# Second layers of the experts by seven products in the second pass, with split weights kept in DRAM by the first

## The chip, the cores and the metric

The kernel runs on one core of a Trainium2 chip. The metric is the device time of one execution in microseconds, from launch to end. Beside it stands one execution with the hardware profiler, whose span runs from the first instruction to the last. The engines are TensorE (PE in the rows; PEld is its loading of weights), VectorE (DVE), ScalarE (ACT), GpSimd (POOL), and SyncE (SP), which here issues every DMA.

## What is computed

An attention with a banded mask gives 2304 tokens of width 512. A mixture of eight experts follows, in which every token passes through every expert, and then a plain block of the same kind. In the reference, cut to what matters:

```python
x = attention(q, k, v)                      # 2304 x 512
P = sinkhorn(exp(x @ w_gate))               # 2304 x 8, weights of the experts
for e in range(8):
    h = np.maximum(x @ w1[e], 0.0)          # 2304 x 1024
    out += P[:, e:e + 1] * (h @ w2[e])      # 2304 x 512
y = np.maximum(out @ w_in, 0.0) ** 2 @ w_out   # hidden width 2048
```

All of it is float32. The matrix engine gets float32 operands in two parts: `hi`, the value cast to a shorter form, and `lo`, the rest. One product of blocks is then three matmuls: hi by hi, hi by lo, lo by hi. Casting `hi` is an ACT instruction, `lo = src - hi` a DVE one.

## The kernel before, in words

After the attention (about the first 100 us) come 80 **steps**: each takes 256 hidden units through both layers. The tokens are cut into two pairs of halves of 512 (tokens 0 to 1023 and 1280 to 2303) and one single block of 256 (1024 to 1279). The steps run in four phases: phase 0, or the **first pass** (steps 0 to 31), takes all experts over the first pair and the single block; phase 1, the **second pass** (steps 32 to 63), takes the same experts over the second pair; phases 2 and 3 (eight steps each, from 64 and 72) do the same for the plain block. Every expert's weights are thus loaded and split twice.

**First layers.** `l1_pair` computes the 2 x 2 block product (two blocks of hidden units, two halves of tokens) by seven block products u1 to u7 instead of eight, from sums and differences of the operands. Its input's combinations lie in slots 0 to 6 of `x_hi`, `x_lo`; those of the weights in `blk` and `sum`. `product` issues six matmuls of 128x512 for each (L473). The results land in the banks `s`, `pt`, `xt`; DVE and ACT put them together, multiply by the tokens' expert weight `pp` (g, L521) and split g into gh and gl (L529, L507).

**Second layers.** `l2_units` returns, for a pair, eight units: four chunks of 128 output channels by two halves of tokens, six matmuls each (L636) into one of three `mm` banks, after which DVE adds the bank to `acc` (L654). The units of step i run between the products of step i+1, so the second layer is one step behind.

**Preparing weights.** `prep_w` in step i makes `blk` and `sum` of step i+1 and `w2` of step i: POOL forms the sums (L146 to L151, four instructions of 128x256), ACT casts three blocks of 128x1024 (L133), and DVE forms three `lo` (L137). Raw weights come by DMA (L119) into the buffers `raw1`, `raw2`.

**Order.** Each engine's instructions run in the order in which they are written down here by hand. `run(u)` writes one unit's matmuls, then everything due; `after(k, f)` makes f due k units later. A unit is the clock: in a step of the second pass the units are u1 u2 u3 u4, then second-layer units and u5, u6, u7 in turn, then the remaining second-layer units.

**Changes of phase.** At the start of a phase the slots of `x_hi` and `x_lo` are filled anew: `new_operands` loads blocks into `xb`, POOL forms differences (L208), ACT and DVE split seven pieces for each of two column blocks j (L211, L214), over the last step of a phase and the first of the next. Before u1 of the new phase `ahead` runs five second-layer units.

**Narrowing.** `w_in` and `w_out` arrive as 64-bit numbers. `narrow` brings a block to float32 in four pieces: a DMA, then 2, 2 and 3 DVE instructions (L176 to L198), and a store to `w32`. There are 32 blocks. `narrow_on` does one piece: two pieces in a step of the first pass, at units 0 and 8, three in a step of the second, at units 0, 5 and 10.

Of the kernel before, what the change touches and what calls it, by code (L numbers as in the profile page):

```python
# [47 lines left out]
def tile_kernel(ctx: ExitStack, tc: tile.TileContext, a):  # L48
# [35 lines left out]
    p_dram = dram.tile([NCH, E, 128], F32, name="p_dram")  # L84

# [15 lines left out]
    wset = [None, None]  # L101

    def new_set(pool, k):
        wset[k] = {
            n: tuple(pool.tile([128, 1024], F32R, name=f"{n}{h}{k}", bufs=1) for h in ("h", "l"))
            for n in ("blk", "sum", "w2")
        }

# [6 lines left out]
    def load_w(i, which):  # L115
        if i >= len(steps):
            return
        dst = raw1.rearrange("p b c -> p (b c)") if which == 0 else raw2
# [6 lines left out]
    def prep_w(i):  # L125
# [16 lines left out]
        if i + 1 < len(steps):  # L142
# [83 lines left out]
    def new_operands(src):  # L226
# [3 lines left out]
        for j, base, loads in ((0, 1, (-6, -6)), (1, 14, (11, 13))):  # L230
# [234 lines left out]
    g_t, acc = {}, {}  # L465

# [65 lines left out]
    def l1_pair(i):  # L532

        bank_a, bank_b, bank_c = bank("s"), bank("pt"), bank("xt")
        made = {}

        def made_here():
            g_t[i, 0] = tuple(
                post[0].tile([128, FC, 2 * T], F32R, tag=n, name=n, bufs=2) for n in ("gh", "gl")
            )  # L540
            for n in ("s2", "s3"):
                made[n] = post[0].tile([128, 512], F32, tag=n, name=n, bufs=1)

        def out(fc, t, src, k):
            gh, gl = g_t[i, 0]
# [32 lines left out]
        def u7():  # L578
            product(bank_c, i, "sum", 3, 2, stop=True)
            after(0, lambda: nc.vector.tensor_tensor(out=made["s2"], in0=bank_c, in1=made["s2"], op=ALU.add))  # L580
            out(0, 1, made["s2"], 2)
# [5 lines left out]
    def l1_single(i):  # L587
        def unit(fcs):

            if fcs[0] == 0:  # L590
                g_t[i, 1] = tuple(
                    post[0].tile([128, FC, NSG], F32R, tag=n, name=n, bufs=1) for n in ("sgh", "sgl")
                )
            gh, gl = g_t[i, 1]
            ps = bank("mm")[:, :len(fcs) * NSG]
# [84 lines left out]

    def operands(i):

        if phase(i) == 1:
            return new_operands(x_dram)
        t0 = PAIRS[pair_of(i)]
        return new_operands(y_dram[:, :, t0:t0 + 2 * T])
# [8 lines left out]
    with tc.manual_schedule():  # L695
# [145 lines left out]
        acc[1] = post[0].tile([128, KC * NSG], F32, name="acc1", bufs=1)  # L841
# [138 lines left out]
```

## Time and profile before

| | |
|---|---|
| median of 3 runs | 1990.86 us (1989.66 to 1990.91) |
| the profiled execution | 1989.59 us |
| its span | 1987.6 us |
| PE busy | 1966.0 us (99%) |
| DVE busy | 1527.3 us (77%) |
| ACT, POOL busy | 711.4, 384.3 us |
| DMA, mean of the span | 80 GB/s |

The profiled execution took 2.0 us more than its span. A busy share counts time in which at least one instruction of the engine is under way. Consecutive matmuls overlap, so that the time of one in the rows is longer than the distance from one to the next. The chain of waits follows the work that ended last back from the end: what stands on it sets the time.

### The profile page before, as it was taken

The numbers are of one execution on the slowest core, as the hardware profiler recorded it, in microseconds if no ns is written. First come the engines' busy times: TensorE is split into PE (matmuls) and PEld (weight loads), VectorE is DVE, ScalarE is ACT, GpSimd is POOL, SyncE is SP. The second block draws the span as 40 slices with busy tenths as digits, with TensorE's granted clock in tenths as the row PEclk, the third lists the DMA queues.
The fourth block names the chain that finished last, engine by engine and source line by source line (L and its number), as shares of the span: only waits on it lengthen the run. The fifth ranks groups of instructions, "written<-read, shape, count | busy, mean of one in ns | idle before, by whom it ended". The sixth has DMA issues, their size and how long they took to land.

```text
span 1987.6 us, 27653 instructions
## 1 busy us (share of the span) xinstructions
PE 1966.0 (99%) x11208; PEld 1634.7 (82%) x11208; DVE 1527.3 (77%) x2272; ACT 711.4 (36%) x1104; POOL 384.3 (19%) x412
## 2 busy tenths in 40 slices
PE   8999999999999999999999999999999999999999
PEld 7778888888888888888888888888888878887887
DVE  5866777777777777778888888888887886678776
ACT  3543223222233333223433333333333354344542
POOL 4621311111110111112212121121212221123120
PEclk9999999999999999999999999999999999999999
DMA  8511111111211111212322222222221221113111
GB/s 291 180 67 61 59 60 57 54 64 64 64 64 64 57 61 53 69 54 100 111 92 83 92 85 95 85 76 90 86 89 59 86 106 43 43 54 109 62 45 51
DMA packets 69807, 158.23 MB, mean 80 GB/s; under 512 B 6176, under 2 KB 31408, under 8 KB 69680
## 3 DMA queue, kind: packets, MB, share of 16 engines
q1 hardware_dynamic: 69680, 156.47, 23.3%
q8 instruction: 88, 1.44, 0.3%
q14 instruction: 39, 0.32, 0.0%
HBM read 136.45 MB, written 20.00 MB: 79 GB/s over the span
## 4 chain that ended last, share of the span: by engine, by line
PE 93%; DVE 5%; ACT 1%; issue 0%; POOL 0%; ACTq 0%; DVEq 0%; POOLq 0%
PE mm L636 47%; PE pt L473 15%; PE s L473 11%; PE xt L473 11%; PE mm L602 6%; PE xt L346 2%; DVE acc L654 1%; PE pt L331 1%; PE mm L773 1%; DVE x_lo L214 1%; PE s L294 1%; DVE blkl L137 1%; DVE g L521 0%; DVE gl L507 0%; DVE suml L137 0%
## 5 line engine op out<-in xcount | busy, mean ns | idle before, releaser
L654 DVE TENSOR_TENSOR acc<-mm,acc 128x512 f32<-128x512 f32 x626 | 429.2, 688 | 156.0 <-PE mm L636 152.9
L529 ACT CAST gh<-g 128x512 fp32r<-128x512 f32 x308 | 191.6, 622 | 585.1 <-DVE g L521 585.1
L636 PE MATMUL mm<-gh,w2h 128*128 128x512 f32 x1024 | 399.5, 390 | 0.9 <-DVE acc L654 0.8
L636 PE MATMUL mm<-gl,w2h 128*128 128x512 f32 x1024 | 398.6, 389 | 0.0
L636 PE MATMUL mm<-gh,w2l 128*128 128x512 f32 x1024 | 398.5, 389 | 0.0
L146 POOL TENSOR_TENSOR sums<-raw 128x256 f32<-128x256 f32 x80 | 66.0, 825 | 1411.5 <-DVE suml L137 1388.3
L636 PEld LDWEIGHTS mm<-gh,w2h 128*128 128x128 f32 x1024 | 192.3, 188 | 43.0 <-DVE acc L654 2.6
L636 PEld LDWEIGHTS mm<-gh,w2l 128*128 128x128 f32 x1024 | 192.2, 188 | 40.1
L636 PEld LDWEIGHTS mm<-gl,w2h 128*128 128x128 f32 x1024 | 192.3, 188 | 39.3
L507 DVE TENSOR_TENSOR gl<-g,gh 128x512 fp32r<-128x512 f32 x308 | 223.3, 729 | 0.0
L521 DVE SCALAR_TENSOR_TENSOR g<-s,pp 128x512 f32<-128x512 f32 x183 | 128.9, 704 | 105.6 <-PE s L473 103.5
L473 PE MATMUL xt<-x_hi,sumh 128*128 128x512 f32 x320 | 125.6, 392 | 0.4
L473 PE MATMUL pt<-x_hi,sumh 128*128 128x512 f32 x320 | 124.8, 390 | 0.8 <-ACT s L566 0.8
L473 PE MATMUL s<-x_hi,blkh 128*128 128x512 f32 x320 | 125.2, 391 | 0.0
L473 PE MATMUL xt<-x_hi,suml 128*128 128x512 f32 x320 | 124.8, 390 | 0.3
L473 PE MATMUL s<-x_lo,blkh 128*128 128x512 f32 x320 | 124.7, 390 | 0.0
L473 PE MATMUL xt<-x_lo,sumh 128*128 128x512 f32 x320 | 124.6, 389 | 0.0
L473 PE MATMUL s<-x_hi,blkl 128*128 128x512 f32 x320 | 124.6, 389 | 0.0
L473 PE MATMUL pt<-x_lo,sumh 128*128 128x512 f32 x320 | 124.5, 389 | 0.0
L473 PE MATMUL pt<-x_hi,suml 128*128 128x512 f32 x320 | 124.5, 389 | 0.0
L602 PE MATMUL mm<-xs,blkh 128*128 128x256 f32 x640 | 115.8, 280 | 0.0
L137 DVE TENSOR_TENSOR w2l<-raw,w2h 128x1024 fp32r<-128x1024 f32 x80 | 102.8, 1285 | 11.6 <-ACT w2h L133 11.6
(146 smaller groups left out, 3634.1 us busy)
## 6 DMA issues: line engine op xcount, KB each, us to landing
raw<-in_w SPq DMA_DIRECT2D x128, 512.0 KB, 3.4
raw<-w SPq DMA_DIRECT2D x32, 512.0 KB, 3.4
v<-in_v SPq DMA_DIRECT2D x24, 384.0 KB, 3.7
pp<-p_dram SPq DMA_DIRECT2D x32, 256.0 KB, 5.7
xb<-in_w_in SPq DMA_DIRECT2D x16, 512.0 KB, 4.6
w<-xb SPq DMA_DIRECT2D x32, 256.0 KB, 2.3
xb<-in_w_out SPq DMA_DIRECT2D x16, 512.0 KB, 4.9
k<-in_k SPq DMA_DIRECT2D x24, 224.0 KB, 4.7
```

The costliest lines, as they stand in the source:

```text
L137: nc.vector.tensor_tensor(out=w[1], in0=src, in1=w[0].bitcast(F32), op=ALU.subtract)
L146: tt(out=c(sums, 0), in0=c(raw1, 2), in1=c(raw1, 3), op=ALU.add)
L214: return lambda: nc.vector.tensor_tensor(out=x_lo[:, k, j], in0=z, in1=x_hi[:, k, j].bitcast(F32), op=ALU.subtract)
L294: nc.tensor.matmul(ps[QB * head:QB * head + QB, 2 * (g % 3) + g // 3, :], qt[rows, pr, g * QB:g * QB + QB], kt[rows, pr, g * QB:g * QB + K ...
L346: nc.tensor.matmul(xt[D * h:D * h + D, pr, c * QB:c * QB + QB], vt[keys, c, head * D:head * D + D], pt[keys, c * 128 + head * QB:c * 128 + ...
L473: nc.tensor.matmul(ps, w[:, c], z[:, x, j], start=start and k == 0, stop=stop and k == 5, skip_group_check=True)
L507: nc.vector.tensor_tensor(out=glo, in0=z, in1=ghi.bitcast(F32), op=ALU.subtract)
L521: nc.vector.scalar_tensor_tensor(out=held["g"], in0=src, scalar=0.0, in1=held["r"], op0=ALU.max, op1=ALU.mult)
L529: after(k + 1, lambda: nc.scalar.copy(ghi, held["g"]))
L602: nc.tensor.matmul(ps[:, n * NSG:n * NSG + NSG], w[:, c], z[:, kc], start=k == 0, stop=k == 3 * KC - 1)
L636: nc.tensor.matmul(ps, lhsT, rhs, start=k == 0, stop=k == 3 * FC - 1)
L654: nc.vector.tensor_tensor(out=dst, in0=ps, in1=dst, op=ALU.add)
```

## The change

The first pass keeps its split weights: `store` writes hi and lo of `blk`, `sum`, `w2` and of a new block `mix` to DRAM (eight DMAs of 512 KB in a step); `fetch` reads them back in the second pass, in which nothing of the experts' weights is loaded raw, summed or split. `mix` holds four sums and differences of blocks of `w2`, formed on POOL in the first pass (m1, m2) and split like the rest.

In the second pass the second layer too is a 2 x 2 block product (two blocks of hidden units by two halves of output channels; two halves of tokens) by seven products v1 to v7 (`l2_mixed`). Each has six matmuls, three into each of two banks. Their operands are made in `out_mixed`: g of the four (block, half) combinations (r1 to r4), four differences on POOL (t1 to t4), and seven splits, named 11, 22, 21 and t1 to t4, where there were four. The result of v1 is copied by ACT from its banks a0, a1 to b0, b1; each of v2 to v7 ends in two adds to `acc` on DVE. The units of a step are in the order `u1 v1 u2 v2 u3 v6 u4 v5 u5 v7 u6 v3 u7 v4`; the v belong to the step before. All eight banks are given out once for the pass.

At the change from phase 1 to 2 `ahead` is empty, and the first units of step 64 are `v1 v2 u1 us v6 v5 u2 ...` (us is the single block's first layer). The pieces of the new operands are due at other units. Narrowing moves: one block in a step of the first pass from step 3, at units 2, 16, 17 and 1 of the next, none in the second pass, the last five blocks in phase 2.

```diff
+    def store(n, s, w):
+        for h, z in zip("hl", w):
+            nc.sync.dma_start(w_dram[n + h][s], z.bitcast(F32))
+    def fetch(n, i, w):
+        for h, z in zip("hl", w):
+            nc.sync.dma_start(z.bitcast(F32), w_dram[n + h][i - NS1])
...
+        if kept(i + 1):
+            w = wset[(i + 1) % 2]
+            out += [(0, lambda: fetch("blk", i + 1, w["blk"])), (0, lambda: fetch("sum", i + 1, w["sum"]))]
...
+        if kept(i):
+            w2 = wset[i % 2]["w2"]
+            out += [(0, lambda: fetch("w2", i, w2)), (0, lambda: fetch("mix", i, mixes[i % 2]))]
...
+            def m1():
+                tt(out=c(z, 0), in0=r[:, 0, 1], in1=r[:, 1, 1], op=ALU.add)
+                tt(out=c(z, 2), in0=r[:, 0, 0], in1=r[:, 0, 1], op=ALU.subtract)
...
+            out += [(1, hi(w2, raw2)), (3, lo(w2, raw2, lambda: store("w2", i, w2)))]
+            out += [(6, m1), (7, m2), (13, hi(m, mix32)), (15, lo(m, mix32, lambda: store("mix", i, m)))]
...
+        def operand(n, src, k, k_lo):
+            b = block[n]
+            after(k, lambda: nc.scalar.copy(b[:, 0], src))
+            after(
+                k_lo,
+                lambda: nc.vector.tensor_tensor(out=b[:, 1], in0=src, in1=b[:, 0].bitcast(F32), op=ALU.subtract),
+            )
...
+                def mix():
+                    sub(r1, r4, r1)
+                    sub(r5, r2, r1)
+                    sub(r4, r2, r4)
+                    sub(r3, r3, r5)
+                after(2, mix)
+                operand("t1", r1, 3, 4)
+                operand("t2", r5, 4, 5)
+                operand("t3", r4, 5, 7)
+                operand("t4", r3, 6, 8)
...
+        def unit(banks, w, n, dst=None, start=False, stop=False, first=False, final=False):
+            z = block[n]
+            for m, ps in enumerate(banks):
+                c = slice(m * 128, m * 128 + 128)
+                for k, (wt, g) in enumerate(((0, 0), (0, 1), (1, 0))):
+                    nc.tensor.matmul(
+                        ps, w[wt][:, c], z[:, g], start=start and k == 0, stop=stop and k == 2, skip_group_check=True
+                    )
+            if dst is None:
+                after(0, lambda: [nc.scalar.copy(o, ps) for o, ps in zip((b0, b1), banks)])
+                return
...
+        return dict(
+            v1=lambda: unit(a_, whole(0, 0), "11", start=True),
+            v2=lambda: unit(a_, whole(1, 0), "21", (0, 0), stop=True, first=True, final=True),
+            v6=lambda: unit(b_, mixed(1), "t2", (0, 1), first=True),
+            v5=lambda: unit(a_, mixed(0), "t1", (1, 1), start=True, first=True),
+            v7=lambda: unit(b_, mixed(2), "t3", (1, 1), final=True),
+            v3=lambda: unit(a_, mixed(3), "22", (0, 1), stop=True, final=True),
+            v4=lambda: unit(b_, whole(1, 1), "t4", (1, 0), stop=True, first=True, final=True),
+        )
...
+                if i == first[2]:
+                    names = "v1 v2 u1 us v6 v5 u2 v7 u3 v3 u4 v4 u5 u6 u7"
+                    u["us"], l1s = l1s[0], []
+                elif i == first[2] - 1:
+                    names = "u1 v1 u2 v2 u3 u4 v6 u5 v5 u6 u7 v7 v3 v4"
+                else:
+                    names = "u1 v1 u2 v2 u3 v6 u4 v5 u5 v7 u6 v3 u7 v4"
...
-                if SCALED + 2 <= i < first[2] - 5 and not slow and k in ((0, 8), (0, 5, 10))[pair_of(i)]:
+                if i >= SCALED and phase(i) in (0, 2) and not slow and done[0] % 4 == {2: 0, 16: 1, 17: 2, 1: 3}.get(k):
                     narrow_on()
```

**PE, inside a step of the second pass, before.** One product of the first layer (u5, into `pt`) and one unit of the second layer behind it (into an `mm` bank; gh, gl are the split g, w2h and w2l the split weights).

```order
L473 MATMUL pt_13254<-x_hi_82,sumh0_142 128x512
L473 MATMUL pt_13254<-x_lo_83,sumh0_142 128x512
L473 MATMUL pt_13254<-x_hi_82,suml0_143 128x512
L473 MATMUL pt_13254<-x_hi_82,sumh0_142 128x512
L473 MATMUL pt_13254<-x_lo_83,sumh0_142 128x512
L473 MATMUL pt_13254<-x_hi_82,suml0_143 128x512
L636 MATMUL mm_13315<-gh_13128,w2h1_2220 128x512
L636 MATMUL mm_13315<-gl_13129,w2h1_2220 128x512
L636 MATMUL mm_13315<-gh_13128,w2l1_2221 128x512
L636 MATMUL mm_13315<-gh_13128,w2h1_2220 128x512
L636 MATMUL mm_13315<-gl_13129,w2h1_2220 128x512
L636 MATMUL mm_13315<-gh_13128,w2l1_2221 128x512
```

**PE, the same place of the changed kernel**: u5 and v7 (g1 holds the operands t2, t3, t4; mixh0 and sg are hi and lo of `mix`; `mm` and `xt` are the banks b0, b1).

```order
L527 MATMUL pt_9251<-x_hi_82,sumh1_2230 128x512
L527 MATMUL pt_9251<-x_lo_83,sumh1_2230 128x512
L527 MATMUL pt_9251<-x_hi_82,suml1_2231 128x512
L527 MATMUL pt_9251<-x_hi_82,sumh1_2230 128x512
L527 MATMUL pt_9251<-x_lo_83,sumh1_2230 128x512
L527 MATMUL pt_9251<-x_hi_82,suml1_2231 128x512
L795 MATMUL mm_9254<-g1_2237,mixh0_2240 128x512 x2
L795 MATMUL mm_9254<-g1_2237,sg_2238 128x512
L795 MATMUL xt_9250<-g1_2237,mixh0_2240 128x512 x2
L795 MATMUL xt_9250<-g1_2237,sg_2238 128x512
```

A second-layer unit still has six matmuls, now three into each of two banks; a step has seven of them where it had eight.

**DVE, from the end of one step of the second pass into the next, before**: adds to `acc` (L654), the three splits of weights (L137), those of g (L507), and narrowing (L176, L180).

```order
L137 TENSOR_TENSOR suml_2219<-sums,sumh_2218 128x1024
L654 TENSOR_TENSOR acc_2222<-mm,acc_2222 128x512
L507 TENSOR_TENSOR gl<-g,gh 128x512
L654 TENSOR_TENSOR acc_2222<-mm,acc_2222 128x512
L521 SCALAR_TENSOR_TENSOR g<-s,pp 128x512
L137 TENSOR_TENSOR w2l_2221<-raw_99,w2h_2220 128x1024
L654 TENSOR_TENSOR acc_2222<-mm,acc_2222 128x512
L507 TENSOR_TENSOR gl<-g,gh 128x512
L137 TENSOR_TENSOR blkl_141<-raw_97,blkh_140 128x1024
L176 TENSOR_SCALAR xb<-xb 128x512
L180 SCALAR_TENSOR_TENSOR xb<-xb 128x512
```

**DVE, the same place of the changed kernel**: s2 of u7 (L681), the lo of 21, g of block 0 and half 1 (L618 into mix), the adds of v4 (L809), the lo of 22, t1 and t2 (L608; the buffers r hold the g and their differences), the adds of v2, g of u3, the lo of t3.

```order
L681 TENSOR_TENSOR s2_10665<-xt_9249,s2_10665 128x512
L608 TENSOR_TENSOR g0_2236<-mix32_2239,g0_2236 128x512
L618 SCALAR_TENSOR_TENSOR mix32_2239<-s2_10665,pp_10207 128x512
L809 TENSOR_TENSOR acc0_2234<-mm_9254,acc0_2234 128x512
L809 TENSOR_TENSOR acc0_2234<-xt_9250,acc0_2234 128x512
L608 TENSOR_TENSOR g0_2236<-r2_9178,g0_2236 128x512
L608 TENSOR_TENSOR g0_2236<-r1_9177,g0_2236 128x512
L608 TENSOR_TENSOR g1_2237<-r5_9179,g1_2237 128x512
L809 TENSOR_TENSOR acc0_2234<-mm_9252,acc0_2234 128x512
L809 TENSOR_TENSOR acc0_2234<-mm_9253,acc0_2234 128x512
L618 SCALAR_TENSOR_TENSOR r1_9177<-s_9247,pp_10643 128x512
L608 TENSOR_TENSOR g1_2237<-mix32_2239,g1_2237 128x512
```

The splits of weights and the narrowing are gone from the step; twelve adds stand where eight stood, and seven splits of operands where four stood, three of them behind differences that POOL forms.

**POOL, over the change from phase 1 to 2, before**: the differences of the new operands (L208) and the sums of weights (L146 to L151).

```order
L208 TENSOR_TENSOR xb<-xb 128x512 x7
L146 TENSOR_TENSOR sums<-raw_97 128x256
L147 TENSOR_TENSOR sums<-raw_97 128x256
L150 TENSOR_TENSOR sums<-sums,raw_97 128x256
L151 TENSOR_TENSOR sums<-raw_97,sums 128x256
L208 TENSOR_TENSOR xb<-xb 128x512
```

**POOL, the same place of the changed kernel**: the differences of the operands t1 to t4 (L629) come between.

```order
L261 TENSOR_TENSOR xb<-xb 128x512 x4
L629 TENSOR_TENSOR r_9177<-mix_2239,r_9177 128x512
L629 TENSOR_TENSOR r_9179<-r_9178,r_9177 128x512
L629 TENSOR_TENSOR mix_2239<-r_9178,mix_2239 128x512
L629 TENSOR_TENSOR mix_2239<-mix_2239,r_9179 128x512
L167 TENSOR_TENSOR sums<-raw_105 128x256
L168 TENSOR_TENSOR sums<-raw_105 128x256
L261 TENSOR_TENSOR xb<-xb 128x512
```

In steps 63 and 64 POOL has four more instructions of 128x512 each than before.

## Rows read from the trace of the kernel before

**Rows 1.** The page: busy time of the engines, and the chain by engine.

```profile
PE 1966.0 (99%) x11208; PEld 1634.7 (82%) x11208; DVE 1527.3 (77%) x2272; ACT 711.4 (36%) x1104; POOL 384.3 (19%) x412
PE 93%; DVE 5%; ACT 1%; issue 0%; POOL 0%; ACTq 0%; DVEq 0%; POOLq 0%
```

**Rows 2.** Windows in first pass, second pass, phase 2: stretch; busy time by engine, clock, DMA.

```profile
500.00:550.00 50.00, 50.00 (x245) 42.39 (x244) 36.13 (x54) 14.40 (x21) 6.64 (x8) 1.00 0.20 64
1200.00:1250.00 50.00, 50.00 (x222) 41.37 (x221) 44.89 (x67) 16.88 (x24) 8.13 (x10) 1.00 0.23 80
1700.00:1750.00 50.00, 50.00 (x237) 42.03 (x237) 34.89 (x50) 20.50 (x32) 7.42 (x8) 1.00 0.12 43
```

**Rows 3.** Chain of waits in the second pass: start, length, engine, bank, line, count.

```profile
1017.02 6.82 PE mm L636 x30
1023.84 1.36 PE s L473 x6
1037.44 6.82 PE mm L636 x30
1179.40 1.67 PE xt L473 x6
1508.82 6.80 PE mm L636 x30
```

**Rows 4.** DVE in order of time, inside a step: start, length, instruction.

```profile
1206.50 0.68 DVE L521 SCALAR_TENSOR_TENSOR g<-s,pp 128x512 f32<-128x512 f32 x1
1207.10 0.69 DVE L654 TENSOR_TENSOR acc<-mm,acc 128x512 f32<-128x512 f32 x1
1207.70 1.22 DVE L137 TENSOR_TENSOR suml<-sums,sumh 128x1024 fp32r<-128x1024 f32 x1
1208.83 0.69 DVE L654 TENSOR_TENSOR acc<-mm,acc 128x512 f32<-128x512 f32 x1
```

**Rows 5.** Groups of instructions, second pass (POOL: all): count, busy us, mean ns, idle before.

```profile
L636 PE MATMUL mm<-gl,w2h 128*128 128x512 f32 x374 | 145.6, 389 | 0.0
L529 ACT CAST gh<-g 128x512 fp32r<-128x512 f32 x93 | 57.8, 622 | 203.2 <-DVE g L521 203.2
L176 DVE TENSOR_SCALAR xb<-xb 128x512 int32<-128x512 int32 x17 | 7.1, 418 | 0.0
L180 DVE SCALAR_TENSOR_TENSOR xb<-xb 128x512 int32<-128x512 int32 x17 | 14.3, 841 | 0.6
L658 POOL TENSOR_TENSOR acc<-acc,pp 128x512 f32<-128x512 f32 x8 | 12.8, 1618 | 15.5 <-DVE acc L654 15.5
```

**Rows 6.** Line L208 on POOL: shortest, median and longest ns.

```profile
L208 POOL TENSOR_TENSOR xb<-xb x24: 1289/1298/2161, 913.5 to 1812.1; 128x512 f32<-128x512 f32 x24
```

**Rows 7.** POOL and DVE in order of time at the change from phase 1 to 2.

```profile
1580.13 2.67 POOL L208 TENSOR_TENSOR xb<-xb 128x512 f32<-128x512 f32 x2 [0.69 <-DVE x_lo L214]
1581.55 2.33 DVE L137 TENSOR_TENSOR w2l<-raw,w2h 128x1024 fp32r<-128x1024 f32 x1
1588.10 2.99 POOL L208 TENSOR_TENSOR xb<-xb 128x512 f32<-128x512 f32 x2 [5.30 <-DVE x_lo L214]
1588.65 1.28 DVE L521 SCALAR_TENSOR_TENSOR g<-s,pp 128x512 f32<-128x512 f32 x1
1589.86 0.68 DVE L654 TENSOR_TENSOR acc<-mm,acc 128x512 f32<-128x512 f32 x1
```

**Rows 8.** Windows of PE alone at that change: stretch, busy, clock, DMA.

```profile
1590.00:1600.00 10.00, 9.19 (x38) 1.00 0.24 70
1600.00:1610.00 10.00, 9.96 (x55) 1.00 0.43 166
```

**Rows 9.** DMA: issues (count, KB, us to landing), and a window like rows 2.

```profile
raw<-in_w SPq DMA_DIRECT2D x128, 512.0 KB, 3.4
y_dram<-acc SPq DMA_DIRECT2D x16, 256.0 KB, 2.1
896.00:898.00 2.00, 2.00 (x10) 1.66 (x9) 1.55 (x3) 0.63 (x2) 0.00 (x0) 1.00 1.00 387
```

More of the change, by code (lines that the diff above doesn't have):

```diff
@@ L115, in load_w @@
     def load_w(i, which):
-        if i >= len(steps):
+        if i >= len(steps) or kept(i):
             return
+        moe, s = steps[i]
+        while not moe and done[0] < 16 * s + 8 * which + 8:
+            narrow_on()
         dst = raw1.rearrange("p b c -> p (b c)") if which == 0 else raw2
@@ L465, in tile_kernel @@
     g_t, acc = {}, {}
+    gbuf, block, r32, own, l2_banks, spare = [], {}, [], {}, [], []
     def product(ps, i, which, slot, x, start=False, stop=False):
@@ L590, in unit @@
             if fcs[0] == 0:
[L591 to L593 removed]
+                g_t[i, 1] = tuple(sg[:, h].rearrange("p (f n) -> p f n", f=FC) for h in range(2))
             gh, gl = g_t[i, 1]
[L595 removed]
+            ps = (spare[0] if i == 2 * NS1 else bank("mm"))[:, :len(fcs) * NSG]
             hi, lo = wset[i % 2]["blk"]
@@ L679, in l2_units, with l2_mixed, add @@
         return [lambda c=c: unit(c, 0, DM) for c in range(n // 128)]
-    def operands(i):
+    def l2_mixed(i):
+        s = steps[i][1]
+        d = acc[0].rearrange("p (e m t n) -> p e m t n", e=2, m=2, t=2)
+        w2 = [z.rearrange("p (f e d) -> p f e d", f=FC, e=2) for z in wset[i % 2]["w2"]]
+        mix = [z.rearrange("p (k d) -> p k d", k=4) for z in mixes[i % 2]]
+        whole = lambda f, e: [z[:, f, e] for z in w2]
+        mixed = lambda k: [z[:, k] for z in mix]
+        (a0, a1), (b0, b1) = l2_banks
+        def unit(banks, w, n, dst=None, start=False, stop=False, first=False, final=False):
[9 more added lines that the diff above has]
+                return
+            def add():
+                e, t = dst
+                for m, ps in enumerate(banks):
+                    o = d[:, e, m, t]
+                    if first and s == 0:
+                        nc.scalar.copy(o, ps)
+                    else:
+                        nc.vector.tensor_tensor(out=o, in0=ps, in1=o, op=ALU.add)
+                    if final and s == NS1 - 1:
+                        t0 = PAIRS[1] + t * T
+                        nc.sync.dma_start(y_dram[:, 2 * e + m, t0:t0 + T], o)
+            after(0, add)
+        a_, b_ = (a0, a1), (b0, b1)
+        return dict(
[6 more added lines that the diff above has]
+            v4=lambda: unit(b_, whole(1, 1), "t4", (1, 0), stop=True, first=True, final=True),
+        )
@@ L865, in tile_kernel @@
                 ahead, l2, l2s = l2[:-3] + l2s, l2[-3:], []
+            if i == NS1 + 1:
+                s0, spare0 = bank("s"), bank("s")
+                x0, x1 = bank("xt"), bank("xt")
+                own.update((k, (s0, bank_p, x0)) for bank_p in [bank("pt")] for k in range(i, 2 * NS1))
+                l2_banks.extend(((bank("mm"), bank("mm")), (bank("mm"), x1)))
+                spare.append(spare0)
             l1 = l1_pair(i) if i else first_units
```

112 lines of the change are left out of this document (88 added, 24 removed).

## The prediction

> **What bounds the kernel now.** The first view is the page: PE is busy for 1966.0 of 1987.6 us and makes up 93% of the chain that ended last [rows 1]. A share that high can hide slack, so the second view is the windows: in the first pass, the second and phase 2 PE is busy for 50.00 of 50.00 us at the full granted clock, while DVE has 36.13, 44.89 and 34.89 us [rows 2]. The reader is to see that in the second pass DVE is the engine nearest to PE. The third view is the chain in order of time, since one matmul is recorded at 389 ns [rows 5] though matmuls overlap. Six matmuls take 1.36 us on it [rows 3], so one costs 0.2267 us; with 389 ns the gain would be overrated by 70%. A step of the second pass has 42 + 48 = 90 matmuls, 20.41 us, and the chain shows 1037.44 - 1017.02 = 20.42. Over 24 steps it shows (1508.82 - 1017.02)/24 = 20.49: some steps lose 0.31 us at u7 (1.67 for six matmuls), where PE waits for DVE [rows 3].
>
> **The matmuls.** The order shows 42 + 42 = 84 matmuls a step. Second-layer units of all 32 steps change: 32 x 6 x 0.2267 = **43.5 us off**, the whole of it on the path as long as PE waits for nothing else. A unit that alternates between two banks is not in the trace; alternate units already change bank after every six matmuls without a loss [rows 3], so I take the same price.
>
> **DVE in a step of the second pass.** Two instructions of 512 columns start 0.60 us apart, one of 1024 holds DVE for 1.13 [rows 4]. Removed: three splits of weights (3.4), an average of three quarters of a narrowing (three instructions of 0.42 and four of about 0.84 make 4.6 [rows 5], so 3.5), eight adds and four splits of g. What stays or is added: twelve adds, seven splits, four g, two sums s2, s3: 25 x 0.60 = **15.0 us in 19.05**. DVE has room, and the 0.07 us a step of waits that narrowing's bursts cause goes: **2 us off** (0 to 2).
>
> **The chain of t2.** An engine with room can still be late in one place. I laid one step out by these prices, with zero at the end of u7 and 1.36 for a unit. v4, u1, v1, u2, v2, u3 take 8.16; then v6 needs the lo of t2 for its second matmul, at 8.39. s2, the lo of 21 and g of (0,1) on DVE end at 2.15. POOL's first difference takes 1.30 [rows 6], to 3.5; DVE meanwhile adds v4 and splits 22, to 4.1. The second difference, t2, ends at 5.3; ACT copies v1's banks from 4.3 to 5.5 (a cast takes 0.62 [rows 5], a copy about as much) and casts t2 to 6.15; POOL's third difference holds the port until 7.1, and the lo of t2 ends at 7.7. That leaves **0.7 us**. The copies end at 5.5, and v2 needs the second bank at 6.1. Later waits (adds of v5 and v7 against v3 and v4) have over 2 us. I price the chain at 0; at what it becomes a stall is a rival below. POOL's four differences (5.2) replace four sums of half the size.
>
> **The port between DVE and POOL.** Where POOL works on two tiles of SBUF, a DVE instruction with two SBUF operands is late: a split that takes 1.22 elsewhere takes 2.33 beside POOL, a g takes 1.28 for 0.69 and POOL's pair 2.99 for 2.67, while an add from a bank stays at 0.68 [rows 7]. In each case DVE's instruction ends about its usual length after POOL's own ended, as if they took turns. The Trainium skill has a rule that speaks against this change: "SBUF — State Buffer", section "SBUF: two separate sides", says that VectorE with two SBUF inputs and GpSimd hold a shared port pair for a whole instruction, and that the other is blocked. The trace agrees (2.33 against 1.22). With turns a steady step still fits, as laid out; the change of phase does not, and the next part's +8 would be +2 if the two merely overlapped.
>
> **The change from phase 1 to 2.** This is the costliest new thing. In step 63 DVE's instructions with two SBUF operands are seven splits of operands, two g, seven x_lo (16 x 0.60) and two of 1024 columns (2.3): 11.9 us. POOL has four differences for the products and four for x (8 x 1.30) and four sums of half the size (estimated at 0.65): 13.0. In turns that is 24.9 in a step whose matmuls take 19.05: 5.9 late. Step 64 has five splits, seven x_lo, two g and three weights: 11.8 + 13.0 = 24.8, against 19.05 + some 2.8 for the single block: 3 late. Before, the same count was 11.2 + 7.8 = 19.0 in 20.4, and PE lost 0.81 + 0.04 us there [rows 8]. ACT also waits, in order, for the second pair of `xb` loads before it can copy v1's banks, and `ahead` no longer covers that. 5.9 + 3 - 0.8 gives **8 us on**. The low bound is 2 (DVE's own 16 x 0.60 + 2.3 + 16 x 0.60 = 21.5 against 19.05); laying the queue out with every such instruction doubled gives 14.
>
> **The first pass and phase 2.** DVE gets one split more (1.13) and half a narrowing more (2.3) in a step; no step is shorter than 20.4, so at most 2.45 x 3.4 = 8.3 us in 50, where 13.9 are free [rows 2]. POOL doubles 6.64 in 50. ACT has two thirds free. Phase 2 takes five narrowings, 23 us, in five steps, with 15 of 50 us free. The units from 14 to 17 get splits and narrowing together, about 1.8 us of DVE for 1.36 of PE, over three units: 1.2 late, which three banks bear. **1 us on**, bounds 0 and 6 (a stall of 0.2 us a step).
>
> **DMA.** In the second pass eight fetches, 4.19 MB, come in 19.05 us: 220 GB/s. In one window the queue moved 387 GB/s at a busy share of 1.00, with PE busy for 2.00 of 2.00 us [rows 9], so a step's fetches need about 11 us and have a whole step. The stores of the first pass add at most 205 GB/s to 64 [rows 2]; a store of 256 KB lands in 2.1 us [rows 9]. Both are hidden: 0. If the cover were gone, see the slower rival. SP issues eight DMAs a step, at which nothing else waits for it.
>
> **Sum.** The profiled execution took 1989.6 (span 1987.6 and 2.0 around it); the runs' median is 1990.86, 1.3 above. 1989.6 - 43.5 - 2 + 8 + 1 = **1953 us**. Bounds of the terms: 1989.6 - 45.5 + 2 = 1946 and 1989.6 - 43.5 + 14 + 6 = 1966; the likely part of it is 1947 to 1960.
>
> **Rivals.**
> - *The chain of t2 is late in each step.* If POOL's differences take 1.62 (POOL's other instruction of 512 columns does on average [rows 5]), two and the third, which holds the port, put the lo of t2 at 8.7: 0.3 us a step, 31 steps: 1962. At 1 us a step 1984. For it: three engines in a row, each in order, with 0.7 us to spare. Against: the shortest and median difference is 1.29 to 1.30 [rows 6].
> - *The change of phase costs little*, because backlog there is caught up under the single block: 1953 - 6 = 1947, with no new waits 1945.
> - *The first pass pays.* Splits, narrowing and stores end the full 50.00 of 50.00: 1 us a step is 27 us, 1980.
> - *Slower: the fetches don't keep up.* One 512 KB load lands 3.4 us after its issue [rows 9]. If eight came one behind another, a step took 27.2 us instead of 20.42: 6.8 x 31 = 211 on, 2200. It decides from 20.42/8 = 2.55 us a fetch. Against it stands the window at 387 GB/s, in which several were under way.
> - *It doesn't do what it says:* the order has 84 matmuls a step; no chance worth a number.
>
> **Chances.** Forecast 0.60 (1947 to 1960); chain of t2 0.18; cheap change of phase 0.10; the first pass pays 0.06; fetches too slow 0.04; others 0.02. The range 1943 to 1975 leaves out the fetches, the upper end of the t2 rival, most of the first pass's and the others: 0.15. A measurement of this kernel tells about 0.2%, 4 us, from no change. Faster 0.94, the same 0.01, slower 0.05.
>
> **What would show it.** Right: steps of the second pass 19.05 us apart on the chain, with no wait of PE for the lo of t2; DVE at 15 to 17 us of a step; PE idle for 5 us or more about step 64; the DMA share near 0.6 in the second pass. A step of 19.3 or more with PE waiting for g or for DVE's splits shows the first rival; PE waiting for a fetch the slower one; first-pass windows under 49.5 of 50 the third. The forecast is wrong if matmuls into alternating banks are more than 0.2267 us apart.

## The result, and where the time went

The changed kernel takes 2010.86 us (median of 4 runs, 2005.66 to 2013.15), the kernel before 1990.88 beside it: a ratio of 1.0098, 95% interval 1.0075 to 1.012. It is slower by 20 us, 1%, where the prediction had 1953 us. The profiled execution took 2008.79 us, its span is 2007.0. The page of the changed kernel, the answer to [rows 1] (engines, then the chain by engine):

```profile
PE 1947.2 (97%) x11016; PEld 1607.5 (80%) x11016; DVE 1701.5 (85%) x2428; ACT 738.5 (37%) x1204; POOL 616.8 (31%) x540
...
PE 73%; DVE 18%; issue 4%; ACT 3%; DMA 1%; SPq 0%; POOL 0%; DVEq 0%; ACTq 0%; POOLq 0%
```

PE has 192 matmuls fewer, 11016, and is busy for 19 us less; yet only 73% of the chain is PE's, where it was 93%, and DVE has 18%. Which stage that is, the windows show. They are those of [rows 2], now of the changed kernel (stretch; busy time and count of PE, PEld, DVE, ACT, POOL; granted clock; DMA share and GB/s):

```profile
500.00:550.00 50.00, 48.43 (x229) 40.10 (x228) 44.49 (x60) 15.63 (x22) 11.84 (x13) 1.00 0.66 229
1200.00:1250.00 50.00, 50.00 (x222) 41.41 (x221) 45.93 (x66) 19.16 (x33) 18.96 (x12) 1.00 0.67 238
1700.00:1750.00 50.00, 50.00 (x245) 42.37 (x244) 43.10 (x63) 19.66 (x31) 7.42 (x8) 1.00 0.19 65
```

The second pass and phase 2 are full, 50.00 of 50.00. The first pass isn't: 229 matmuls are left of 245. To add up the stages I read where the first matmul of u1 starts in a step. First the kernel before, steps 5, 32 and 63, then the changed one (one matmul into tile `s`: ns, start):

```profile
L473 PE MATMUL s<-x_hi,blkh x1: 395/395/395, 234.5 to 234.5; 128*128 128x512 f32 x1
...
L473 PE MATMUL s<-x_hi,blkh x1: 474/474/474, 947.6 to 947.6; 128*128 128x512 f32 x1
...
L473 PE MATMUL s<-x_hi,blkh x1: 389/389/389, 1576.7 to 1576.7; 128*128 128x512 f32 x1
```

```profile
L527 PE MATMUL s<-x_hi,blkh x1: 395/395/395, 253.9 to 253.9; 128*128 128x512 f32 x1
...
L527 PE MATMUL s<-x_hi,blkh x1: 481/481/481, 994.2 to 994.2; 128*128 128x512 f32 x1
...
L527 PE MATMUL s<-x_hi,blkh x1: 389/389/389, 1580.4 to 1580.4; 128*128 128x512 f32 x1
```

With steps 0, 65 and the ends of the spans read in the same way:

| stretch | before | after | difference | predicted |
|---|---|---|---|---|
| up to u1 of step 0 (attention) | 109.3 | 114.3 | +5.0 | 0 |
| steps 0 to 4 | 125.2 | 139.6 | +14.4 | with the next row: |
| steps 5 to 31 | 713.1 | 740.3 | +27.2 | +1 |
| steps 32 to 62 | 629.1 | 586.2 | -42.9 | 30 x -1.36 - 2 = -42.8 |
| steps 63 and 64 | 45.4 | 59.8 | +14.4 | 2 x -1.36 + 8 = +5.3 |
| steps 65 to the end | 365.5 | 366.8 | +1.3 | 0 |
| sum | 1987.6 | 2007.0 | +19.4 | -36.5 |

The gain came as predicted. More than that was lost ahead of the second pass (46.6 us, 5.0 of them in the attention) and in steps 63 and 64 (14.4). The rows rest on one profile of each kernel; the attention's differs between profiles of the same kernel by as much as it does here, as the last experiments on it show.

**A step of the first pass** took 25.98 us before and takes 27.07. One step in order of time, at its first units; the columns are start, length, engine, line, instruction and, in brackets, idle time with what ended it. DVE, POOL, ACT and PE of the changed kernel:

```profile
551.73 1.11 DVE L233 SCALAR_TENSOR_TENSOR xb<-xb 128x512 int32<-128x512 int32 x1
552.87 0.85 DVE L237 TENSOR_SCALAR xb<-xb 128x512 int32<-128x512 int32 x1
553.75 1.11 DVE L240 SCALAR_TENSOR_TENSOR xb<-xb 128x512 f32<-128x512 int32 x1
...
555.84 1.11 DVE L247 SCALAR_TENSOR_TENSOR xb<-xb 128x512 f32<-128x512 uint32 x1
...
557.59 0.68 DVE L575 SCALAR_TENSOR_TENSOR g<-s,pp 128x512 f32<-128x512 f32 x1
...
551.49 0.80 POOL L172 TENSOR_TENSOR sums<-raw,sums 128x256 f32<-128x256 f32 x1
552.25 1.19 POOL L199 TENSOR_TENSOR mix<-raw 128x256 f32<-128x256 f32 x1
...
555.55 0.85 POOL L204 TENSOR_TENSOR mix<-raw,mix 128x256 f32<-128x256 f32 x1
...
558.30 0.62 ACT L583 CAST g<-g 128x512 fp32r<-128x512 f32 x1 [2.55 <-DVE g L575]
558.83 0.58 ACT L667 COPY s<-pt 128x512 f32<-128x512 f32 x1
...
555.80 0.39 PE L527 MATMUL pt<-x_hi,sumh 128*128 128x512 f32 x1
...
559.46 0.50 PE L527 MATMUL pt<-x_hi,sumh 128*128 128x512 f32 x1 [0.79 <-ACT s L667]
```

The reader follows one piece of lateness through three engines. POOL works through sums and mix in one go, since mix needs only the raw weights, and that is where the narrowing now stands. Beside it the four instructions of the narrowing shown here take 0.85 to 1.11 us; in the first pass of the kernel before, the same lines took 0.42 us (those that read one tile) and 0.69 (two tiles), and the 0.84 of [rows 5] is already the longer mean of the second pass. So DVE reaches g of (0,0) at 557.59, though u3 was done at about 556 (u4 begins at 555.80). ACT's cast waits for that g. Behind the cast, in ACT's order, stands the copy of s2, which has nothing to do with g, and PE's u5 waits for the copy: 0.79 us idle, and six matmuls in 1.66 instead of 1.36. That is the 1.09 of a step, 22 times of 22 in the waits from 300 to 900 us (who waited for whom: us in total, times, longest):

```profile
PE pt L527 <- ACT s L667: 17.3, 22, 0.8
```

**Steps 0 to 4** hold two larger stalls. Step 4 (33.67 us, before 26.02) has the same wait, but of 4.7 us, since the instructions that scale `acc` once stand at the same place. What PE does after it is dear too. The chain of the changed kernel there, and one window:

```profile
231.33 0.49 ACT s L667
...
231.87 2.93 PE pt L527 x6
234.79 2.56 PE mm L735 x6
237.35 1.58 PE pt L527 x6
```

```profile
231.00:236.00 5.00, 4.13 (x10) 3.27 (x11) 3.14 (x4) 1.40 (x3) 0.00 (x0) 0.50 0.90 303
```

After the wait the granted clock is 0.50, the lower of the two levels (1.2 GHz), and six matmuls take 2.93, 2.56 and 1.58 us where 1.36 is their price: 3.0 us more on top of 4.7.

Step 1 (35.67, before 28.42) waits for a load. ACT, and SP's issues, of the changed kernel in order of time:

```profile
141.75 1.04 ACT L151 CAST w2h<-raw 128x1024 fp32r<-128x1024 f32 x1 [8.74 <-DMA raw<-in_w]
...
130.27 0.33 SPq L137 DMA_DIRECT2D raw<-in_w  x1
...
131.67 1.44 SPq L118 DMA_DIRECT2D w_sumh<-sumh  x1
...
134.54 1.17 SPq L137 DMA_DIRECT2D raw<-in_w  x1
```

The load of w2 is issued at 134.54, behind four stores, and lands at 141.72, 7.2 us later, where 3.4 was usual before [rows 9] and 5.9 is the median of such loads in the changed kernel. ACT's cast waits for it, and behind the cast again the copy of s2.

**Steps 63 and 64.** Windows of the changed kernel:

```profile
1590.00:1600.00 10.00, 5.88 (x23) 4.18 (x23) 10.00 (x12) 3.25 (x6) 6.74 (x6) 0.98 0.17 54
1600.00:1610.00 10.00, 7.17 (x24) 5.07 (x24) 10.00 (x14) 5.29 (x9) 5.69 (x5) 0.84 0.32 105
1610.00:1620.00 10.00, 7.83 (x21) 5.76 (x20) 9.99 (x11) 5.58 (x9) 7.91 (x7) 0.50 0.06 24
...
sum 60.00, PE 49.54 PEld 37.32 DVE 58.89 ACT 27.49 POOL 33.58; mean PE 8.26 PEld 6.22 DVE 9.82 ACT 4.58 POOL 5.60
```

(The sum is over six windows, 1580 to 1640.) DVE has no gap for 50 us, with 11 to 14 instructions in 10 us, and PE waits; then the clock falls to 0.50 as well. The chain of the changed kernel over this stretch:

```profile
1577.82 1.37 PE xt L527 x6
...
1579.22 0.69 DVE s L681
...
1633.20 0.61 DVE g L575
...
1634.99 1.68 PE pt L527 x6
```

Between 1579.2 and 1633.8 no piece of it is PE's: all are DVE's, or issue. What PE loses there by its lower clock lies beside DVE's work and not on the chain.

**Phase 3** loses 0.4 us a step (20.8 for 20.4). The chain of the changed kernel:

```profile
1909.83 1.22 DVE suml L155
...
1911.10 1.20 PE xt L527 x4
```

The lo of sum moved from unit 12 to 14. In phase 3 a step has 15 units, 14 is the last, and the next step's u2 waits for it.

### The profile page after: what moved, and what is told of

It reads as the page before. It is cut to its first block, busy times and chain, and to the rows that moved or that the text cites. A ratio compares the mean times of both kernels' runs of the same rounds, so it can differ in the third digit from the quotient of the medians.

```text
span 2007.0 us, 28899 instructions
## 1 busy us (share of the span) xinstructions
PE 1947.2 (97%) x11016; PEld 1607.5 (80%) x11016; DVE 1701.5 (85%) x2428; ACT 738.5 (37%) x1204; POOL 616.8 (31%) x540
## 4 chain that ended last, share of the span: by engine, by line
PE 73%; DVE 18%; issue 4%; ACT 3%; DMA 1%; SPq 0%; POOL 0%; DVEq 0%; ACTq 0%; POOLq 0%
PE mm L735 25%; PE pt L527 14%; PE mm L795 11%; PE xt L527 8%; PE s L527 6%; PE xt L795 3%; DVE acc L749 2%; PE xt L399 2%; DVE xb L233 2%; DVE xb L247 2%; DVE xb L240 2%; DVE suml L155 2%; PE mm L701 1%; DVE xb L229 1%; DVE xb L237 1%
## 5 line engine op out<-in xcount | busy, mean ns | idle before, releaser
L735 PE MATMUL mm<-g,w2h 128*128 128x512 f32 x1024 | 318.4, 392 | 0.0
L167 POOL TENSOR_TENSOR sums<-raw 128x256 f32<-128x256 f32 x48 | 42.8, 892 | 789.6 <-DVE suml L155 676.9
L583 ACT CAST g<-g 128x512 fp32r<-128x512 f32 x180 | 111.8, 621 | 333.7 <-DVE g L575 333.7
L735 PEld LDWEIGHTS mm<-g,w2h 128*128 128x128 f32 x1024 | 193.5, 189 | 40.6
L735 PE MATMUL mm<-g,w2l 128*128 128x512 f32 x512 | 200.2, 391 | 0.0
L809 DVE TENSOR_TENSOR acc<-mm,acc 128x512 f32<-128x512 f32 x282 | 183.7, 677 | 0.0
L629 POOL TENSOR_TENSOR r<-mix,r 128x512 f32<-128x512 f32 x32 | 42.2, 1318 | 402.4 <-DVE mix L618 370.9
L735 PE MATMUL mm<-w2h,g 128*128 128x512 f32 x512 | 157.8, 389 | 0.4 <-DVE acc L753 0.4
L608 DVE TENSOR_TENSOR g<-r,g 128x512 fp32r<-128x512 f32 x128 | 147.1, 1150 | 12.6 <-ACT g L605 4.6
L527 PE MATMUL xt<-x_hi,sumh 128*128 128x512 f32 x320 | 125.2, 391 | 2.4 <-DVE s L672 2.4
L527 PE MATMUL s<-x_lo,blkh 128*128 128x512 f32 x320 | 125.2, 391 | 0.0
L561 DVE TENSOR_TENSOR g<-g,g 128x512 fp32r<-128x512 f32 x180 | 124.5, 699 | 0.0
L605 ACT CAST g<-mix 128x512 fp32r<-128x512 f32 x96 | 59.7, 622 | 167.3 <-DVE mix L618 102.7
L795 PE MATMUL mm<-g,mixh 128*128 128x512 f32 x384 | 119.2, 391 | 0.3 <-DVE g L608 0.3
```

The lines of the kernel that those rows point to most:

```text
L167: tt(out=c(sums, 0), in0=c(raw1, 2), in1=c(raw1, 3), op=ALU.add)
L527: nc.tensor.matmul(ps, w[:, c], z[:, x, j], start=start and k == 0, stop=stop and k == 5, skip_group_check=True)
L561: nc.vector.tensor_tensor(out=glo, in0=z, in1=ghi.bitcast(F32), op=ALU.subtract)
L583: after(k + 1, lambda: nc.scalar.copy(ghi, held["g"]))
L605: after(k, lambda: nc.scalar.copy(b[:, 0], src))
L608: lambda: nc.vector.tensor_tensor(out=b[:, 1], in0=src, in1=b[:, 0].bitcast(F32), op=ALU.subtract),
```

## The experiments

The theory after these readings: narrowing beside POOL's block makes DVE late, and ACT's order hands that to PE; loads behind stores cost step 1 and the attention; DVE in turns with POOL is the bound of steps 63 and 64. The rivals: the traffic of the stores (229 GB/s in all, before 64), or simply too many DVE instructions. Where no range stands beside a time, the kernel ran once, with the profiler.

**One copy moved.** ACT's copy of s2 ahead of its cast:

```diff
         def u4():
             product(bank_b, i, "sum", 1, 5)
-            after(0, lambda: nc.scalar.copy(made["s2"], bank_b))
+            nc.scalar.copy(made["s2"], bank_b)
```

> ACT's copy of s2 is written ahead of its cast of g(0,0), whose input comes from DVE; the rest is unchanged. Theory (narrowing makes DVE late at g, and ACT's order hands that on to PE's u5): PE's wait of 0.8 us for the copy goes, steps 5 to 29 fall from 27.07 to 26.0 to 26.3 us and step 4 from 33.7 to 26 to 28; the run falls by 25 to 35 us, to about 1980. Rival (DVE simply has too much to do in a step, 24.2 us with the waits for the port): PE waits elsewhere, for adds or for g of a later product, and the steps stay at 26.7 or more. Rival (the traffic of the stores): steps stay at 27.07.

Measured: 1972.88 us, with the kernel before at 1993.73 on the same chip. Steps 5 to 30 take 25.98; step 4 takes 29.07, a little more than was expected. A window of this kernel:

```profile
500.00:550.00 50.00, 50.00 (x245) 42.38 (x244) 46.53 (x62) 17.01 (x24) 15.88 (x16) 1.00 0.67 238
```

DVE has all its work and its lateness, 46.53 of 50, the DMA moves 238 GB/s, and PE loses nothing. The loss in steps 5 to 31 was the order of two instructions on an engine that is idle for two thirds. Timed again, over four runs:

> The same kernel as the earlier run with ACT's copy of s2 ahead of its cast, timed in rounds against the kernel before. Expected: 1970 to 1976 us, 0.988 to 0.992 of the kernel before; if that single look was luck, 2000 or more.

Measured: 1974.12 us, ratio 0.9909 (0.9886 to 0.9931) to the kernel before.

**Narrowing in the middle.**

```diff
-  done[0] % 4 == {2: 0, 16: 1, 17: 2, 1: 3}.get(k)
+  done[0] % 4 == {2: 0, 8: 1, 10: 2, 12: 3}.get(k)
```

> The narrowing's four pieces in a step of the first pass (and phase 2) are due at units 2, 8, 10 and 12 instead of 2, 16, 17 and 1 of the next. Theory: beside POOL's eight instructions at the ends of steps the narrowing's own take 0.86 to 1.11 us instead of 0.42 to 0.69; in the middle they take the short times, g(0,0) is in time, steps 5 to 29 fall from 27.07 to 25.98 to 26.1 us, step 4 to below 28, the run by 30 to 35 us, to about 1976. Rival (too much work for DVE): the adds of the middle are late, PE waits for mm banks or for g, and steps stay at 26.6 or more.

Measured: 2003.53 us; steps 5 to 29 take 26.81 to 26.89. Waits from 300 to 900 us of this kernel:

```profile
PE mm L735 <- DVE acc L753: 12.2, 22, 0.6
```

The narrowing's instructions do take the short times there, 0.42 and 0.69 us, so the turns are gone. But in the middle DVE has an add to `acc` at every unit and is full: with narrowing among them the add that frees an `mm` bank is late, once in each step. The rival held here: away from POOL the old wait is gone, and a new one of nearly the same size is there; a step is 0.2 us shorter, no more.

**POOL's differences for mix left out, all else kept.**

```diff
             def m1():
+                if i:
+                    return
                 tt(out=c(z, 0), in0=r[:, 0, 1], in1=r[:, 1, 1], op=ALU.add)
```

(m2 likewise, but for its load.)

> From step 1 on POOL's four differences for mix are left out of the first pass; ACT's cast, DVE's split and the stores of mix stay (of stale values), and so does narrowing. Theory (turns at the port): POOL's block at the ends of steps shrinks from 6.6 to some 3 us, the narrowing's last four instructions fall from 0.85 to 1.11 us to 0.45 and 0.69, 1.7 us in all, as much as g(0,0) is late: steps 5 to 29 take 25.98 to 26.2 us. Rival (DVE's own instructions, mixl among them, are what is too much): steps stay at 26.7 or more.

Measured: 1977.83 us, steps 5 to 30 at 25.98. Groups of DVE from 300 to 900 us (count; busy us, mean ns; idle before), first the changed kernel, then this one, in which the same two lines are three further down:

```profile
L240 DVE SCALAR_TENSOR_TENSOR xb<-xb 128x512 f32<-128x512 int32 x22 | 24.5, 1115 | 0.8
L237 DVE TENSOR_SCALAR xb<-xb 128x512 int32<-128x512 int32 x22 | 18.6, 845 | 0.8
```

```profile
L243 DVE SCALAR_TENSOR_TENSOR xb<-xb 128x512 f32<-128x512 int32 x23 | 15.9, 692 | 0.8
L240 DVE TENSOR_SCALAR xb<-xb 128x512 int32<-128x512 int32 x23 | 12.4, 539 | 0.8
```

DVE's instructions are the same in number. Without POOL's mix beside them these are shorter by 0.3 to 0.4 us each, and that is enough. At this place it is the turns, not the count; in the middle of the step, where there are no turns, the count alone made a wait. And with the copy ahead of the cast the late g costs PE nothing: the lateness comes from the turns, and PE's wait needs ACT's order as well.

**The block mix left out altogether.**

```diff
-            out += [(6, m1), (7, m2), (13, hi(m, mix32)), (15, lo(m, mix32, lambda: store("mix", i, m)))]
+            out += [(7, lambda: load_w(i + 1, 1))]
```

> The block mix is left out of the first pass: POOL's four differences, ACT's cast, DVE's split, two stores (the second pass fetches w2 in its place); stores of the rest and narrowing stay where they are. POOL's block at the ends of steps is then 2.8 us instead of 6.6 and DVE has 1.4 us less there. Theory (turns at the port stretch the narrowing's instructions): they fall from 0.86 to 1.11 us to near 0.42 and 0.69 in part, g(0,0) is in time and steps 5 to 29 take 25.98 to 26.2 us. Rival (narrowing at this place is too much for DVE even without turns): steps stay at 26.6 or more.

Measured: 25.98 a step, 1973.94 us. It agrees, but by itself couldn't tell turns from count.

**No stores.**

```diff
-        for h, z in zip("hl", w):
+        for h, z in zip("hl", w if s == NS1 - 1 else ()):
```

> The first pass stores the split weights of its last step only, and every fetch of the second pass reads these; all else of the changed kernel is left. The stores' traffic (some 160 GB/s) goes, DVE's, ACT's and POOL's work stays. Theory (narrowing beside POOL's block makes DVE late at g, ACT's order hands it on): steps 5 to 29 stay at 27.0 to 27.1 us; the attention loses its 5 us (first layer at 109 to 110); step 1 falls from 35.7 to about 30, as the load of w2 is short but still stands late in the queue; the run is 10 to 12 us shorter, 1997. Rival (the traffic, by late landings and crowded memory, is what costs the steps): steps fall to 25.98 and the run to 1970.

Measured: 2000.33 us, steps 5 to 29 at 27.07, step 1 at 30.47, u1 of step 0 at 111.0. A window of this kernel:

```profile
500.00:550.00 50.00, 49.21 (x240) 41.16 (x238) 45.17 (x61) 15.64 (x22) 15.90 (x16) 1.00 0.22 69
```

With 69 GB/s instead of 229 a steady step is as long as with the stores: the traffic costs it nothing. The whole run came out 3 us above what was expected, the attention 1 to 2. Step 1 is another matter.

**The load of w2 ahead of the stores in step 0.**

```diff
-            out += [(6, m1), (7, m2), (13, hi(m, mix32)),
+            out += [(6 if i else 3, m1), (7 if i else 4, m2), (13, hi(m, mix32)),
```

> In step 0 alone POOL's mix is written at units 3 and 4 instead of 6 and 7, so that the load of step 1's w2 stands ahead of the stores of blk and sum in SP's queue. Theory: step 1 takes 35.7 us instead of 28.4 because ACT waits 8.7 us for that load, and behind ACT's cast stand the copy of s2 and PE's u5: step 1 falls to 28 to 29 us, the run to 2002. Rival: the load is slow for the traffic of the stores, wherever it stands in the queue: step 1 stays above 33 us.

Measured: step 1 takes 31.35 us, 2002.99 in all. That is 4.3 us less than in the changed kernel, of the 7.3 that were lost. But in the ten other runs that keep the stores and leave this load where it was, step 1 takes 33.4 to 36.5 us, so the load's place in the queue is worth 2 to 5 us, and no closer figure is shown. For the rest, the chain of this kernel:

```profile
130.01 1.22 DVE suml L155
131.23 1.14 DVE mixl L155
...
136.32 0.42 DVE scs L479
...
136.78 0.60 PE mm L485 x2
137.38 2.76 PE pt L527 x6
```

Step 0 has seven units, so everything due later in it comes at the last. The lo of mix there lies ahead of the short DVE instructions of sinkhorn, PE waits for these (2.4 us, as in the changed kernel; 0.9 in the kernel before), and its clock falls again (six matmuls in 2.76).

**Step 0's stores behind the attention.**

```diff
-                if i + 1 < NS1:
+                if i < 0:
+                    held_back.append(lambda: store(n, 0, w[n]))
+                elif i + 1 < NS1:
                     store(n, i + 1, w[n])
```

> The four stores of step 0's split weights (blk and sum, hi and lo) are issued behind the attention instead of among its loads; nothing else changes. Theory: they share the queue with q, k and v, these land late, PE waits at 62 to 67 us and its clock falls to 0.5: the first layer of step 0 then starts at 109.3 us as before, not at 114.3, and the run is 5 us shorter than the changed kernel, 2004. Rival: the 5 us are chance or come from the layout of memory: the start stays at 114 and the run at 2009. The steps of the first pass stay at 27.07 us in either case.

Measured: 2001.75 us, u1 of step 0 at 109.2. But over all profiles that start scatters from 112.4 to 119.6 with the stores among the attention's loads and from 109.2 to 113.5 without, so it was run again, beside the changed kernel:

> The changed kernel itself, unaltered, beside the next run on the same chip. Over the runs so far the first layer starts at 112.4 to 119.6 us where step 0's stores lie among the attention's loads (nine profiles) and at 109.2, 111.0 and 113.5 where they don't (three), so that the 5 us may be partly chance. Expected: 2005 to 2015 us, a start at 112 to 116.

> The kernel with step 0's four stores behind the attention, timed on the same chip as the changed kernel. If these stores cost the attention its time: 4 to 5 us less than the changed kernel in the medians, and a start at 109 to 111. If the attention's time is chance: medians within 2 us of each other.

Measured: 2007.63 us (six runs, 2002.88 to 2011.03) for the changed kernel and 2002.82 (2001.41 to 2010.14) with the late stores; but the profiled run of the latter, its slowest, starts u1 at 117.7. The median is 4.8 us shorter and the spread of the single runs is as large. The medians speak for the stores as a cause; but the 95% intervals of the two ratios to the kernel before overlap (1.0050 to 1.0091 and 1.0037 to 1.0077), so it isn't shown.

What the profiles do show is that a late start goes with a low clock of PE. Over the first 109 us the mean granted clock is 0.98 and 0.97 in the two that start earliest (109.2, and 109.3 of the kernel before), 0.92 in the changed kernel's at 114.3, and 0.92, 0.89 and 0.89 in the three that start last (118.1, 119.6, and 117.7 with the late stores). Which waits of the attention bring the clock down in one execution and not in the next was not taken apart, and so the 5.0 us stay open.

**Steps 63 and 64 without POOL's differences.**

```diff
         def sub(o, x, y):
-            return lambda: nc.gpsimd.tensor_tensor(out=o, in0=x, in1=y, op=ALU.subtract)
+            return lambda: None if not diffs else nc.gpsimd.tensor_tensor(out=o, in0=x, in1=y, op=ALU.subtract)
```

> At the change from phase 1 to 2 POOL's eight differences of the new operands are left out (the operands of phase 2 are then not the sums they should be); ACT's and DVE's seven splits for each column block stay. In the changed kernel steps 63 and 64 take 59.8 us for 41 us of matmuls. Theory (turns between DVE and POOL): 10 us of POOL's work gone take 8 to 10 us off, the two steps take 50 to 52 us. Rival (DVE's own number of instructions is the bound): they stay at 57 or more. The first pass is unchanged, 27.07 us a step.

Measured: 53.5 us for the two steps, 6.3 less. A window of this kernel:

```profile
1604.00:1624.00 20.00, 13.33 (x68) 10.51 (x67) 20.00 (x27) 10.89 (x18) 9.82 (x8) 1.00 0.27 83
```

Between the two expectations: DVE does 27 instructions in 20 us instead of 25, but is still never idle. Turns with these eight explain a third of what the two steps wait.

**The operands of phase 2 made ahead.**

```diff
+    def fetch_x(slot):
+        for h, z in ((0, x_hi), (1, x_lo)):
+            nc.sync.dma_start(z[:, slot].bitcast(F32), x2_dram[slot, h])
...
+            if i == first[2] - 1:
+                for n, slot in zip((0, 2, 4, 5, 7, 9, 10), (0, 4, 1, 5, 6, 3, 2)):
+                    after(n, lambda slot=slot: fetch_x(slot))
```

> The operands of phase 2 are made in the second pass, one of fourteen every second step (load of y, difference on POOL, cast, split, two stores of 256 KB); at the change SP fetches them straight into x_hi and x_lo as each slot comes free, fourteen loads of 512 KB, and DVE, ACT and POOL have nothing to do for it. Theory (DVE with its turns is the bound of the change): steps 63 and 64 take 43 to 46 us instead of 59.8, the second pass stays at 19.04 to 19.1 a step, and the run is 14 to 17 us shorter, 1993. Rival (the order of the units there, or the fetches): PE waits for a slot's load, since step 63 then moves some 10 MB, 27 us at 387 GB/s, and the two steps stay above 52 us.

Measured: 50.8 us for the two steps, 1997.04 in all, with the second pass at 19.04 a step. Windows of this kernel:

```profile
1577.40:1597.40 20.00, 19.41 (x85) 15.42 (x83) 19.69 (x27) 9.45 (x15) 12.65 (x10) 1.00 0.95 374
1597.40:1607.40 10.00, 5.55 (x16) 3.86 (x15) 9.37 (x11) 4.85 (x8) 8.64 (x7) 0.78 0.64 261
```

9 us of 19 are gone, neither theory's number. Over the first 20 of the 29 us of step 63 PE is now busy, at 374 GB/s; then it waits once, 4.1 us, for ACT's copy of v1, which waits for DVE's adds, and pays with the clock. DVE still takes turns with POOL's four t and four sums. What is left was not taken apart further.

**All together**, with the lo of sum at unit 12 outside the first pass.

```diff
-            out += [(10, hi(w["sum"], flat(sums))), (14, lo(w["sum"], flat(sums), lambda: keep("sum")))]
+            out += [(10, hi(w["sum"], flat(sums))), (14 if i + 1 < NS1 else 12, lo(w["sum"], flat(sums), lambda: keep("sum")))]
```

> Five edits at once: the late stores of step 0, the early load of step 1's w2, ACT's copy ahead of its cast, the operands of phase 2 made in the second pass, and the lo of sum back at unit 12 in phases 2 and 3 (in the changed kernel PE's second product of a step of phase 3 waits for it, 20.8 us a step instead of 20.4). If the causes are separate, the gains add: from the 1972.9 us of the run with the copy alone, 3 for the attention, 5 for step 1, 9 for steps 63 and 64 and 2 for phase 3 go, to 1954 (1950 to 1959), 0.98 of the kernel before. If DVE is the one bound behind them all, one edit uncovers the next wait and the sum falls short: 1962 or more.

Measured: 1955.56 us (1954.04 to 1959.32), ratio 0.9814 (0.9789 to 0.9839) to the kernel before. The page of this kernel:

```profile
PE 1923.5 (98%) x11016; PEld 1602.9 (82%) x11016; DVE 1691.0 (86%) x2428; ACT 741.2 (38%) x1204; POOL 617.2 (32%) x540
...
PE 92%; DVE 5%; ACT 1%; DMA 1%; issue 1%; POOL 0%; ACTq 0%; DVEq 0%; POOLq 0%
```

The chain is PE's again. The gains nearly add: steps 5 to 30 at 25.98, step 1 at 29.82, 63 and 64 at 49.1, phase 3 at 20.40; the attention of the profiled run is not among them (u1 at 113.5).

## Why the prediction was wrong

The table's sum came out 55.9 us above the forecast's: 40.6 of them in steps 0 to 31, 9.1 in steps 63 and 64, 5.0 in the attention, 1.3 at the end.

- **The matmuls: right.** Steps of the second pass are 19.04 us apart, 0.2267 a matmul, also into alternating banks; -42.9 for -42.8.
- **The chain of t2: it is in time, and the rival with 0.18 was not the case.** Steps 34 to 60 take 19.04 us each, although POOL's four differences take 1.32 to 1.74 us on average in the second pass, where the working had 1.30 and the rival laid 0.3 us of loss on 1.62. In the trace's step at 1200 us the lo of t2 ends 7.3 us after u7, where the working had 7.7: its second difference, ending at 5.3, started at 4.0, and in the trace it starts at 3.5. One duration was too short and one wait too long; that they cancelled is luck. DVE is busy for 17.5 us of a step, just above the 15 to 17 given.
- **"The first pass and phase 2: 1 us on" failed**, and with it the chances: the rival "the first pass pays", 1 us a step, had 0.06 and was the case, with its own sign, a first-pass window under 49.5 of 50 (48.43); of its three causes the stores had no part. Two steps of the working failed. First, it set DVE's added 3.4 us a step against 13.9 free in 50. The addition was 5.4 (DVE is busy for 46.53 us in 50 with the copy moved, 36.13 before [rows 2], in steps of 25.98). DVE did have room even so, but work has a place: a burst is late for what stands behind it, whatever the mean. It did look at the burst, "1.2 late, which three banks bear", and stopped there: the banks bore it, g of the next step did not, and from g it went over ACT's order to u5. Secondly, the narrowing was priced at 0.42 and 0.84 us an instruction [rows 5], where beside POOL's block it takes up to 1.11. The working had found the turns in [rows 7] and used them in the second pass and for steps 63 and 64, but not here, though POOL's block doubled exactly where narrowing was put.
- **"Both are hidden: 0" was right in steady steps** (no stores: still 27.07), wrong at the start, where a load stands behind stores in SP's one queue (2 to 5 us of step 1). GB/s said nothing about that; the order of SP's issues would have. The attention had no term at all; whether the stores cost it anything is open.
- **The change of phase was mis-sized:** 8, bounds 2 and 14, measured 17: 59.8 us for 2 x 84 x 0.2267 + 2.85 = 40.9 of matmuls leave 18.9 of waiting, before 1.8. DVE was the bound, as the working said, but its sum, 24.9 + 24.8 = 49.7, held only POOL's work and DVE's instructions with two SBUF operands, and let all others of DVE, adds above all, run beside POOL for nothing. The 70 instructions that DVE starts from 1580 to 1640 come to 44.7 us at the working's own 0.60 and 1.13; it was busy for 58.9. By this estimate turns stretched it by some 14 us, about half of POOL's 26 by the working's prices, and the gap from 49.7 to 58.9 is the gap from 8 to 17.
- **No term for the clock anywhere.** In step 4 a wait of 4.7 us cost 7.7.

The range ended at 1975, because the first pass was given 1 us, and its own rival too small a chance.

## What to carry to other kernels

Room in an engine's busy time is no price for added work: put the work into the order, with the durations of its neighbours there, and follow its lateness through each in-order engine, to instructions that have nothing to do with it, until it meets slack or PE. Where a wait shows, look first at the order on the engine that was waited for: here one line, a copy ahead of a cast, was worth as much as leaving out a whole block of the work. And a queue that gets stores must be read for the loads behind them, at the start of the program above all.

## What was unexpected of the hardware

A DVE instruction with a single operand was stretched beside POOL too: the narrowing's TENSOR_SCALAR took 0.845 us on average, 0.539 with half of POOL's block gone, and 0.421 with the narrowing in the middle of the step, away from POOL (the first of these instructions took 0.418 before [rows 5]). The prediction had counted instructions with two SBUF operands only. The Trainium skill, "SBUF — State Buffer", section "SBUF: two separate sides", names both as users of the shared port pair: VectorE with two SBUF inputs and VectorE in a two-port performance mode; the trace agrees, if that is the mode that these ran in, which no row says.

The granted clock fell to 0.50 after waits of 2.4 to 4.7 us, and what followed took up to twice its time for some 5 us (2.93, 2.56, 1.58 for 1.36). The first 110 us scatter by several microseconds between profiles of the same kernel (114.3 and 118.1 for the changed one, 109.2 and 117.7 with the late stores), which is more than some of the effects looked for there.
